# Two last stages of an attention-and-MLP kernel: the order of seven products per unit, the accumulators of the next unit, and the tile of one sum

## The chip, the cores and the metric

The kernel runs on one core of one Trainium2 chip. The metric is the device time of one launch in microseconds (us). A core has five engines that run side by side and meet only through semaphores: TensorE (PE) for matrix products, VectorE (DVE), ScalarE (ACT), GpSimd (POOL), and SyncE (SP), which here only issues transfers. [...]

## The reference, cut to what matters

Eight batches of eight heads (576 positions, head dimension 64) go through an attention with a forgetting gate; the 4608 rows of 512 values that come out go through an MLP of 2048 hidden features with a tanh GELU.

```python
attn = softmax(scale * q @ k.T + decay, causal)     # per batch and head
x    = (attn @ v)  as [4608, 512]
h    = x @ w_in                                     # [4608, 2048]
g    = 0.5 * h * (1 + tanh(c * (h + 0.044715 * h**3)))
out  = g @ w_out                                    # [4608, 512]
```

## The kernel before

The rows are worked in nine chunks of 512, numbered 0 to 8. For each chunk there are an input half (`x @ w_in` and GELU, into the tile `gT`) and an output half (`g @ w_out`, `seven_products`, lines from 554). Attention for later rows is interleaved with the MLP of earlier ones. The order of all work is written out by hand: `TABLES[c]` holds one string for chunk c, whose words are played from left to right, and each engine runs its instructions in the order in which they are issued. From chunk 7 on no attention is left: the tables of chunks 7 and 8 hold only MLP work.

The words that matter here:

- `F.n`, `O.n`: the next n steps of the output half of this chunk, or of the chunk before (a step is one matmul; `f.n` plays each as four narrow ones).
- `P.pr` and `p.pr`: the input half of a pair of feature tiles by plain products (eight matmuls of 512 columns); `p` plays it in two halves of four matmuls, the second with its GELU (lines 384 to 392). It has a PSUM tile of its own.
- `R.k.act`: the next step of unit k (`seven_in`, a generator; each `yield` ends a step). In chunks 7 and 8 three units, 1, 0 and 3, run one after the other, all with act 1.
- `T`: `x_sums` for the next chunk, four DVE subtractions (line 406) that make the operands t1 to t4.
- `K.k.n` and `k.k.n`: one of the four sums of weights of unit k (`w_sums`, line 421), on DVE or on POOL. The fourth overwrites a block of `w_in_sb` and is the operand s3.
- `G`: sums of parts of `gT` on DVE for the output half. `D`: softmax denominators (a transpose, a reciprocal, a transpose, on DVE).

A unit makes four output blocks (two feature tiles by 256 columns each) with seven products of four matmuls instead of eight. I name the products by the accumulator: `pa` and `pb` come from the pool `psS` (two slots), `pc` and `pd` from `psM` (two slots).

| name | product | line that issues it | what follows, and on which engine |
|---|---|---|---|
| A1 | a11 b11 into `pa` | 444 | P: ACT copies `pa` to SBUF, 447 |
| B | s2 t2 into `pb` | 451 | U = pb + P on DVE, 452 |
| C1 | s1 t1 into `pc` | 453 | V = pc + U on DVE, 454 |
| D1 | s3 t3 into `pd` | 455 | W = pd + V on DVE, 456; GELU of W on ACT, 462 |
| A2 | a12 b21 added into `pa` | 459 | GELU straight from `pa` on ACT, 460 |
| C2 | s4 b22 added into `pc` | 463 | X = pc + U on DVE, 464; GELU of X, 477 |
| D2 | a22 t4 added into `pd` | 468 | Y = pd + U on DVE, 474; GELU of Y, 480 |

C2 and D2 accumulate onto what C1 and D1 left, so C2 may start only when V has read `pc`, D2 only when W has read `pd`, and A2 only when P has been copied. U, V and W are a chain on DVE. X is written into P's tile and Y into U's tile, so Y waits for X. The number on a name is its unit's (W0 is W of unit 0, P3 the copy of unit 3). In the profile the matmuls of all products have the line 433, all GELUs of a unit 442. H0 and H1 are the two halves of `p.2`, between products of the units; `p.6` gives two more around unit 3's last two products.

The order on PE in chunk 7 is: A1 B C1 D1 A2 (unit 1), H0, C2 D2 (unit 1), A1 B C1 D1 A2 (unit 0), H1, C2 D2 (unit 0), A1 B C1 D1 A2 (unit 3), a half of `p.6`, C2, D2, the other half, then the output half. ACT's order around unit 0 and 3 is: GELU of A2 of unit 0, GELU of the pair of `p.2`, GELU of W0, copy P3, GELU of X0 and Y0, and so on. In chunk 8 unit 1's A1 is issued ahead of the last ten matmuls of chunk 7's output half; all else is as in chunk 7.

The pool `psS` gives a new tile the slot that has been free longest. Built, unit 0's `pa` lies in the bank that unit 1's `pb` had, and its `pb` in that of unit 1's `pa`; unit 3's are turned once more.

Of the kernel before, what the change touches and what calls it, by code (L numbers as in the profile page):

```python
# [16 lines left out]
def kernel(  # L17
# [10 lines left out]
    nc = tc.nc  # L28

    B, H, S, D = q.shape  # L30
# [76 lines left out]
    """  # L107
    TABLES[6] = """
        Y O.512 P.0.1 R.1 P.4.1 R.1 R.1 LK.q5 LQ.q5 M.q2.2 LV R.3.4 P.2.1 R.3 R.3 G.0.1.2 P.6 R.3 G.0.3.4 K.0.0 K.0.1 K.0.2 G.1.1.2 X F.10 S.q3.0 D.q2
        M.q3.0 f.22 S.q3.1 V.q2.0 M.q3.1 VW.q3 f.18 S.q3.2 V.q2.1 M.q3.2 cl.q3 k.0.3 f.20 D.q3 f.18 V.q3.0 v.q3.1 T f.14  # L110
    """
    TABLES[7] = """
        Y O.512 R.1.1 R.1 p.2 R.1 R.1 R.0.1 R.1 R.0 p.2 R.0 R.0 R.3.1 R.0 R.3 p.6 R.3 R.3 p.6 R.3 G.0.1.2 G.1.1.2 G.0.3.4 F.40 T
    """
    TABLES[8] = """
        O.62 R.1.1 O.512 R.1 p.2 R.1 R.1 R.0.1 R.1 R.0 p.2 R.0 R.0 R.3.1 R.0 R.3 p.6 R.3 R.3 p.6 R.3 G.0.1.2 G.1.1.2 G.0.3.4
    """

    singles = ctx.enter_context(tc.tile_pool(name="singles", bufs=1))
# [8 lines left out]
    def many(n, shape, dtype, name):  # L128
        return [singles.tile(shape, dtype, name=f"{name}{i}") for i in range(n)]
# [16 lines left out]
    u1, u2, u4 = many(3, [128, HF, HD], BF16, "usum")  # L146
# [249 lines left out]
    def x_blocks(c):  # L396

        new, old = xT[:, :, CH * c:CH * (c + 1)], xT[:, :, CH * (c - 1):CH * c]
        return [z[:, 2 * a:2 * a + 2, HC * b:HC * (b + 1)] for z in (new, old) for a in range(2) for b in range(2)]

    def x_sums(c, which, eng):

        b11, b12, b21, b22, t1, t2, t3, t4 = x_blocks(c)
        todo = ((t1, b12, b11), (t2, b22, t1), (t4, b21, t2), (t3, b22, b12))
        for k in which:
            eng.tensor_sub(*todo[k])

    def w_blocks(k):

        n = 256  # L410
        a11, a12, a21, a22 = (w_in_sb[:, 2 * b:2 * b + 2, HU * a + n * k:HU * a + n * (k + 1)]
                              for a in range(2) for b in range(2))
        old = xT[:, :, CH * HOMES[k]:CH * (HOMES[k] + 1)]
        return a11, a12, a21, a22, old[:, 0:2, 0:n], old[:, 0:2, n:], old[:, 2:4, 0:n]
# [5 lines left out]
        for n in which or range(4):  # L420
            (eng.tensor_sub if n else eng.tensor_add)(*todo[n])

    def seven_in(c, k, act=0):

        a11, a12, s3, a22, s1, s2, s4 = w_blocks(k)
        b11, b12, b21, b22, t1, t2, t3, t4 = x_blocks(c)
        pa, pb = (psS.tile([128, 2, 512], FP32, name="ps_ab", tag="s")[:, 0].rearrange("p (j n) -> p j n", j=2) for _ in range(2))
        pc, pd = (psM.tile([128, 2, HC], FP32, name="ps_cd", tag="m") for _ in range(2))

        def multiply(ps, w, x, first):  # L430
            for j in range(2):
                for dt in range(2):
                    nc.tensor.matmul(ps[:, j], w[:, dt, 128 * j:128 * j + 128], x[:, dt],  # L433
                                     start=(first and j == 0 and dt == 0), stop=(dt == 1),
                                     skip_group_check=True)

        def part():
            return snap_pool.tile([128, 2, HC], FP32, name="snap", tag="snap")

        def gelu(i, j, x):  # L440
            ft = N_FT // 2 * i + 2 * k
            nc.scalar.activation(gT[:, ft:ft + 2, HC * j:HC * (j + 1)], x, AF.Gelu_apprx_tanh)  # L442

        multiply(pa, a11, b11, True)
        p1, u2, v4 = part(), part(), part()
        if act in (1, 2, 3):
            nc.scalar.copy(p1, pa)
            yield
        else:
            nc.vector.tensor_copy(p1, pa)  # L450
        multiply(pb, s2, t2, True)
        nc.vector.tensor_add(u2, pb, p1)
        multiply(pc, s1, t1, True)
        nc.vector.tensor_add(v4, pc, u2)
        multiply(pd, s3, t3, True)
        nc.vector.tensor_add(v4, pd, v4)  # L456
        if act == 4:
            yield
        multiply(pa, a12, b21, False)
        gelu(0, 0, pa)  # L460
        yield
        gelu(1, 1, v4)
        multiply(pc, s4, b22, False)
        nc.vector.tensor_add(p1, pc, u2)
        if act in (0, 3, 4):
            gelu(0, 1, p1)
        yield
        multiply(pd, a22, t4, False)
        if act == 2:
            z = part()  # L470
            nc.scalar.copy(z, pd)
            nc.gpsimd.tensor_add(u2, z, u2)
        else:
            nc.vector.tensor_add(u2, pd, u2)
        if act in (1, 2):
            yield
            gelu(0, 1, p1)
        if act == 2:
            yield
        gelu(1, 0, u2)  # L480
        yield

    def mlp_in_half(half, g, spare=0):
# [252 lines left out]
    def load_values(b, half):  # L736
# [41 lines left out]
        "f": lambda c, n: out_part(c, n, 1),  # L778
        "K": lambda k, *which: w_sums(k, nc.vector, which),
        "T": lambda c, *which: x_sums(c, which or range(4), nc.vector),  # L780
        "B": keep_busy,
        "X": load_exp,
# [16 lines left out]
    def quads(call):  # L799
# [7 lines left out]
        "f": lambda c, n: out_part(c, n, 1),  # L807
        "P": lambda c, pr, spare=0: mlp_in(c, (pr,), spare),
        "R": lambda c, k, *how: next(units.setdefault((c, k), seven_in(c, k, *how))),
        "p": lambda c, pr: next(halves.setdefault((c, pr), mlp_in_halves(c, pr))),  # L810
        "TT": lambda c, *which: x_sums(c, which or range(4), nc.vector),
        "T": lambda c, *which: x_sums(c + 1, which or range(4), nc.vector),
        "t": lambda c, *which: x_sums(c + 1, which or range(4), nc.gpsimd),
        "G": lambda c, half, *which: gelu_sums(half, which or (1, 3, 2, 4)),
# [48 lines left out]
```

## Time and profile before

| what | value |
|---|---|
| median of 3 runs | 320.69 us (320.36 to 320.79) |
| the profiled execution | 320.23 us, span 318.5 us, mean granted TensorE clock 0.999 |
| PE, DVE, ACT, POOL busy, share of the span | 98%, 79%, 65%, 36% |
| chunk 7, from unit 1's A1 to the output half | 263.88 to 277.27 us |
| chunk 8, from unit 1's B to the output half | 289.94 to 302.53 us |

Times within the span count from its start. A row of the timeline gives the start, the duration, the engine, the line and the tiles of an instruction or of several equal ones in a row (x4). A matmul of 256 columns is shown with 0.27 us, though the next one starts 0.109 us later, because matmuls are pipelined: whether PE stood still is read from the distance of starts and not from its busy share. Four such matmuls, one product, take 0.4365 us from start to start (264.31, 264.75, 265.19 for three products in a row), four of 512 columns 0.865 us.

### The profile page before, as it was taken

What the parts mean: (1) busy time and instruction counts of PE and PEld (TensorE: products, weight loads), DVE (VectorE), ACT (ScalarE), POOL (GpSimd) and SP (SyncE); (2) the same over time, 40 slices, a digit from 0 to 9 for tenths busy, and PEclk for the clock granted to TensorE, in tenths of its full rate; (3) what the DMA queues carried; (4) which work ended last, traced back from release to release, by engine and by line L of the source; (5) the groups of instructions that cost most, each with busy time, mean ns of one, the idle gap of its engine ahead of it and who ended that gap; (6) DMA issues with size and microseconds to landing.
All of it is one profiled execution on the core that took longest, in us unless ns stands there. A gap on an engine that the chain in (4) does not pass through costs nothing.

```text
span 318.5 us, 12369 instructions
## 1 busy us (share of the span) xinstructions
PE 310.9 (98%) x5533; PEld 218.8 (69%) x5553; DVE 251.5 (79%) x402; ACT 206.1 (65%) x260; POOL 115.2 (36%) x163
## 2 busy tenths in 40 slices
PE   7999999999999999999999999999999999999995
PEld 3468744445876577767867777768776798788784
DVE  6877059877788999779977999689868978886882
ACT  4894767677756786659665965778477834722730
POOL 8996476910500229501870078105710350000000
PEclk9999999999999999999999999999999999999999
DMA  7999999898114820791159413961120111003013
GB/s 128 226 209 192 206 217 234 160 204 177 37 37 121 142 65 7 155 227 19 37 104 212 87 37 81 182 140 37 37 68 0 37 39 66 3 33 102 0 35 99
DMA packets 47574, 33.45 MB, mean 105 GB/s; under 512 B 29857, under 2 KB 42273, under 8 KB 47521
## 3 DMA queue, kind: packets, MB, share of 16 engines
q0 software_dynamic: 9712, 15.99, 29.2%
q1 hardware_dynamic: 37664, 16.60, 19.7%
q8 instruction: 43, 0.70, 1.0%
q14 instruction: 11, 0.08, 0.1%
q10 hardware_dynamic: 144, 0.07, 0.1%
HBM read 36.85 MB, written 9.44 MB: 145 GB/s over the span
## 4 chain that ended last, share of the span: by engine, by line
PE 94%; DMA 2%; DVE 1%; issue 1%; ACT 1%; POOL 0%; DVEq 0%; ACTq 0%; POOLq 0%
PE ps_w L567 30%; PE ps_h L374 16%; PE po L329 9%; PE ps_s L262 9%; PE ps_cd L433 8%; PE ps_ab L433 6%; PE pso L639 4%; PE ps_h L493 4%; PE ps_h L388 2%; DMA q_c<-in_q_dram 2%; PE po_m L315 1%; PE ps_q L516 1%; ACT pt L270 1%; PE idle_ps L240 1%; PE ps_o L329 0%
## 5 line engine op out<-in xcount | busy, mean ns | idle before, releaser
L270 ACT ACTIVATE pt<-ps_s 128x1024 bf16<-128x1024 f32 (+2 forms) x98 | 92.3, 992 | 36.2 <-PE ps_s L262 32.7
L276 POOL TENSOR_SCALAR_AFFINE_SELECT pt<-pt 128x512 bf16<-128x512 bf16 (+2 forms) x69 | 41.0, 603 | 102.9 <-ACT pt L270 101.8
L374 PE MATMUL ps_h<-xT,w_in_sb 128*128 128x512 bf16 x228 | 54.5, 379 | 0.6
L567 PEld LDWEIGHTS <-gT 128*32 128x32 bf16 (+1 forms) x1247 | 50.5, 97 | 6.1 <-issue 1.7
L567 PE MATMUL ps_w<-w_out_sb,gT 128*32 128x256 bf16 (+1 forms) x1050 | 46.9, 273 | 0.0
L381 ACT ACTIVATE gT<-ps_h 128x1024 bf16<-128x1024 f32 x30 | 30.6, 1021 | 19.5 <-PE ps_h L374 19.2
L567 PEld LDWEIGHTS <-gsum 128*32 128x32 bf16 (+1 forms) x1256 | 39.2, 97 | 1.4
L374 PEld LDWEIGHTS <-w_in_sb 128*128 128x128 bf16 x240 | 23.4, 98 | 24.3 <-issue 0.4
L262 PE MATMUL ps_s<-qT,kT 32*128 32x448 bf16 (+5 forms) x880 | 35.3, 261 | 0.3 <-DVE qT L198 0.2
L215 POOL TENSOR_TENSOR vw<-v_nat,wT 128x1280 bf16<-128x1280 f32 (+1 forms) x13 | 29.8, 2292 | 3.2 <-DVE xT L360 2.8
L567 PE MATMUL ps_w<-usum,gsum 128*32 128x256 bf16 (+1 forms) x832 | 30.6, 273 | 0.0
L198 DVE STREAM_TRANSPOSE kT<-k_c 128x576 f32<-128x576 f32 x16 | 19.9, 1243 | 11.6 <-DMA k_c<-in_k_dram 11.6
L592 DVE TENSOR_TENSOR o_st<-ps_w,snap 128x512 f32<-128x512 f32 x31 | 21.2, 686 | 8.8 <-PE ps_w L567 7.7
L433 PEld LDWEIGHTS <-w_in_sb 128*128 128x128 bf16 x240 | 23.4, 98 | 6.7 <-issue 1.0
L442 ACT ACTIVATE gT<-snap 128x512 bf16<-128x512 f32 x45 | 26.1, 626 | 2.9 <-DVE snap L456 2.4
L262 PEld LDWEIGHTS <-kT 32*128 32x128 bf16 x896 | 16.0, 92 | 17.1 <-issue 12.2
L329 PE MATMUL po<-pt,vw 128*32 128x64 bf16 (+4 forms) x624 | 22.6, 278 | 0.0
L360 DVE TENSOR_TENSOR xT<-po,rb 128x576 bf16<-128x576 f32 x26 | 19.5, 751 | 3.1 <-PE po L329 2.7
L329 PEld LDWEIGHTS <-vw 128*32 128x32 bf16 x672 | 14.2, 97 | 10.4 <-issue 4.1
L433 PEld LDWEIGHTS <-xT 128*128 128x128 bf16 x180 | 17.6, 98 | 4.4
L198 DVE STREAM_TRANSPOSE qT<-q_c 128x576 f32<-128x576 f32 x16 | 19.9, 1245 | 0.7 <-DMA q_c<-in_q_dram 0.6
L433 PE MATMUL ps_cd<-xT,w_in_sb 128*128 128x256 bf16 x120 | 18.0, 272 | 0.3 <-DVE snap L456 0.3
(112 smaller groups left out, 475.3 us busy)
## 6 DMA issues: line engine op xcount, KB each, us to landing
out_dram<-o_st SPq DMA_DIRECT2D x35, 256.0 KB, 2.6
k_c<-in_k_dram POOLq DMA_DIRECT2D x16, 288.0 KB, 5.9
q_c<-in_q_dram POOLq DMA_DIRECT2D x16, 288.0 KB, 7.1
v_nat<-in_v_dram SPq DMA_DIRECT2D x16, 256.0 KB, 6.5
v_nat<-in_v_dram SPq DMA_DIRECT2D x20, 128.0 KB, 5.6
w_in_sb<-in_moe_w_in_dram POOLq DMA_DIRECT2D x8, 256.0 KB, 6.7
w_out_sb<-in_moe_w_out_dram POOLq DMA_DIRECT2D x4, 512.0 KB, 10.2
v_nat<-in_v_dram POOLq DMA_DIRECT2D x9, 128.0 KB, 7.9
```

The source lines that it names most:

```text
L198: nc.vector.transpose(out=dst.rearrange("p s c -> p (s c)").bitcast(FP32) .rearrange("p (t a) -> p a t", a=S // 32), in_=src.rearrange("p ...
L215: return eng.tensor_mul(vw[i % 2][:, t0:t1], vb[:, t0:t1, h0:h0 + 4, :], wT[:, i, t0:t1, :].unsqueeze(3).to_broadcast([128, t1 - t0, 4, D]))
L262: nc.tensor.matmul(tiles[h // 2][:, h % 2, c0:c0 + nq], key_columns(i, key, h, c), qq[32 * h:32 * h + 32, q0:q0 + nq, c], start=(c == 0 an ...
L270: nc.scalar.activation(p[:, 2 * g:2 * g + 2, off:off + n], t[:, :, 0:n], AF.Exp, scale=scale)
L276: nc.gpsimd.affine_select(out=x, in_=x, compare_op=ALU.is_ge, fill=0.0, base=0, pattern=pattern, channel_multiplier=-1)
L329: nc.tensor.matmul(po[r0:r0 + w.shape[-1], 448 + q0:448 + q0 + nq], w, p[:, h, col:col + nq], start=(key in (0, "low")), stop=(key in ("lo ...
L374: nc.tensor.matmul(ph[:, j, :], w_in_sb[:, dt, 128 * ft:128 * ft + 128], xT[:, dt, CH * c:CH * (c + 1)], start=(dt == 0), stop=(dt == N_DT ...
L381: nc.scalar.activation(gT[:, 2 * pr:2 * pr + 2, :], ph, AF.Gelu_apprx_tanh)
L433: nc.tensor.matmul(ps[:, j], w[:, dt, 128 * j:128 * j + 128], x[:, dt], start=(first and j == 0 and dt == 0), stop=(dt == 1), skip_group_c ...
L442: nc.scalar.activation(gT[:, ft:ft + 2, HC * j:HC * (j + 1)], x, AF.Gelu_apprx_tanh)
L567: nc.tensor.matmul(ps[c0:c0 + width, n, cols[0]:cols[1]], x[:, j, 128 * n + c0:128 * n + c0 + width], w[:, j, cols[0]:cols[1]], start=(fir ...
L592: nc.vector.tensor_add(st, ps, kept[name])
```

## The change

Six edits, of which the first four concern chunks 7 and 8 (act 1) alone:

1. In a unit, A2 and its GELU are issued ahead of D1 and W.
2. P and U share a tile (U is written over P); X and Y each have a tile of their own, so Y no longer waits for X.
3. Unit 0's A1, with its copy, is issued between unit 1's C2 and D2, and unit 3's between unit 0's C2 and D2.
4. Unit 0 swaps the names of its two `psS` tiles. Built, every accumulator lies in the same bank as before.
5. In all chunks, `x_sums` makes t3 third and t4 fourth (before: t4 third, t3 fourth).
6. In chunk 6, the fourth weight sum of unit 0 moves from POOL to DVE and behind 20 steps of the output half; on DVE it stands between an addition of the output half (line 592) and the transpose of a denominator (line 348).

```diff
@@ TABLES[6], the second line
-        ... M.q3.2 cl.q3 k.0.3 f.20 D.q3 f.18 V.q3.0 v.q3.1 T f.14
+        ... M.q3.2 cl.q3 f.20 K.0.3 D.q3 f.18 V.q3.0 v.q3.1 T f.14
@@ TABLES[7]
-        Y O.512 R.1.1 R.1 p.2 R.1 R.1 R.0.1 R.1 R.0 p.2 R.0 R.0 R.3.1 R.0 R.3 p.6 R.3 R.3 p.6 R.3 G.0.1.2 G.1.1.2 G.0.3.4 F.40 T
+        Y O.512 R.1.1 R.1 p.2 R.1 R.0.1.1 R.1 R.1 R.0 p.2 R.0 R.3.1 R.0 R.0 R.3 p.6 R.3 R.3 p.6 R.3 G.0.1.2 G.1.1.2 G.0.3.4 F.40 T
@@ TABLES[8]
-        O.62 R.1.1 O.512 R.1 p.2 R.1 R.1 R.0.1 R.1 R.0 p.2 R.0 R.0 R.3.1 R.0 R.3 p.6 ...
+        O.62 R.1.1 O.512 R.1 p.2 R.1 R.0.1.1 R.1 R.1 R.0 p.2 R.0 R.3.1 R.0 R.0 R.3 p.6 ...
@@ x_sums
-        todo = ((t1, b12, b11), (t2, b22, t1), (t4, b21, t2), (t3, b22, b12))
+        todo = ((t1, b12, b11), (t2, b22, t1), (t3, b22, b12), (t4, b21, t2))
@@ seven_in
-    def seven_in(c, k, act=0):
+    def seven_in(c, k, act=0, swapped=0):
...
+        if swapped:
+            pa, pb = pb, pa
...
         multiply(pa, a11, b11, True)
-        p1, u2, v4 = part(), part(), part()
+        p1 = part()
+        u2, v4 = (p1, None) if act == 1 else (part(), part())
...
         multiply(pc, s1, t1, True)
+        v4 = v4 or part()
         nc.vector.tensor_add(v4, pc, u2)
+        if act == 1:
+            multiply(pa, a12, b21, False)
+            gelu(0, 0, pa)
         multiply(pd, s3, t3, True)
         nc.vector.tensor_add(v4, pd, v4)
         if act == 4:
             yield
-        multiply(pa, a12, b21, False)
-        gelu(0, 0, pa)
+        if act != 1:
+            multiply(pa, a12, b21, False)
+            gelu(0, 0, pa)
         yield
         gelu(1, 1, v4)
         multiply(pc, s4, b22, False)
-        nc.vector.tensor_add(p1, pc, u2)
+        c12 = part() if act == 1 else p1
+        nc.vector.tensor_add(c12, pc, u2)
...
         multiply(pd, a22, t4, False)
...
-            nc.vector.tensor_add(u2, pd, u2)
+            c21 = part() if act == 1 else u2
+            nc.vector.tensor_add(c21, pd, u2)
```

The number of matmuls, of weight loads and of transfers is the same, and so is ACT's order. DVE has one instruction more and POOL one less.

More of the change, by code (lines that the diff above doesn't have):

```diff
@@ L109 @@
         Y O.512 P.0.1 R.1 P.4.1 R.1 R.1 LK.q5 LQ.q5 M.q2.2 LV R.3.4 P.2.1 R.3 R.3 G.0.1.2 P.6 R.3 G.0.3.4 K.0.0 K.0.1 K.0.2 G.1.1.2 X F.10 S.q3.0 D.q2
-        M.q3.0 f.22 S.q3.1 V.q2.0 M.q3.1 VW.q3 f.18 S.q3.2 V.q2.1 M.q3.2 cl.q3 k.0.3 f.20 D.q3 f.18 V.q3.0 v.q3.1 T f.14
+        M.q3.0 f.22 S.q3.1 V.q2.0 M.q3.1 VW.q3 f.18 S.q3.2 V.q2.1 M.q3.2 cl.q3 f.20 K.0.3 D.q3 f.18 V.q3.0 v.q3.1 T f.14
     """
     TABLES[7] = """
-        Y O.512 R.1.1 R.1 p.2 R.1 R.1 R.0.1 R.1 R.0 p.2 R.0 R.0 R.3.1 R.0 R.3 p.6 R.3 R.3 p.6 R.3 G.0.1.2 G.1.1.2 G.0.3.4 F.40 T
+        Y O.512 R.1.1 R.1 p.2 R.1 R.0.1.1 R.1 R.1 R.0 p.2 R.0 R.3.1 R.0 R.0 R.3 p.6 R.3 R.3 p.6 R.3 G.0.1.2 G.1.1.2 G.0.3.4 F.40 T
     """
     TABLES[8] = """
-        O.62 R.1.1 O.512 R.1 p.2 R.1 R.1 R.0.1 R.1 R.0 p.2 R.0 R.0 R.3.1 R.0 R.3 p.6 R.3 R.3 p.6 R.3 G.0.1.2 G.1.1.2 G.0.3.4
+        O.62 R.1.1 O.512 R.1 p.2 R.1 R.0.1.1 R.1 R.1 R.0 p.2 R.0 R.3.1 R.0 R.0 R.3 p.6 R.3 R.3 p.6 R.3 G.0.1.2 G.1.1.2 G.0.3.4
     """
@@ L463, in seven_in @@
         multiply(pc, s4, b22, False)
-        nc.vector.tensor_add(p1, pc, u2)
+        c12 = part() if act == 1 else p1
+        nc.vector.tensor_add(c12, pc, u2)
         if act in (0, 3, 4):
-            gelu(0, 1, p1)
+            gelu(0, 1, c12)
         yield
@@ L471, in seven_in @@
             nc.scalar.copy(z, pd)
-            nc.gpsimd.tensor_add(u2, z, u2)
-        else:
-            nc.vector.tensor_add(u2, pd, u2)
+            c21 = u2
+            nc.gpsimd.tensor_add(c21, z, u2)
+        else:
+            c21 = part() if act == 1 else u2
+            nc.vector.tensor_add(c21, pd, u2)
         if act in (1, 2):
             yield
-            gelu(0, 1, p1)
+            gelu(0, 1, c12)
         if act == 2:
             yield
-        gelu(1, 0, u2)
+        gelu(1, 0, c21)
         yield
```

## The prediction

> **What bounds the kernel now.** I read the shares of the engines first, then the chain that ended last, then the timelines of PE, ACT and DVE in chunks 7 and 8, where the change lies.
>
> The page's busy times and, from the chain, the one stretch of chunks 7 and 8 that is not PE:
>
> ```profile
> PE 310.9 (98%) x5533; PEld 218.8 (69%) x5553; DVE 251.5 (79%) x402; ACT 206.1 (65%) x260; POOL 115.2 (36%) x163
> ...
> 270.25 0.88 PE ps_h L388 x4
> 271.15 0.70 DVE snap L456
> 272.50 0.87 PE ps_ab L433 x8
> ```
>
> PE carries the chain, so only time in which PE stands still can be won, and the reader should see that there is little. Work without a gap in chunk 7 would be 21 products of 0.4365 us and four halves of 0.865 us, 12.63 us; it took 277.27 - 263.88 = 13.39. Chunk 8 from unit 1's B: 20 products and four halves, 12.19 us, against 302.53 - 289.94 = 12.59. So 0.76 and 0.40 us, 1.16 in all, is the most that the order can give.
>
> Where it lies, in chunk 7, from the timelines of PE, ACT and DVE (H1, C2 and D2 of unit 0; GELU of the pair, GELU of W0, copy P3; then V0, W0, X0):
>
> ```profile
> 270.08 1.03 PE L388 MATMUL ps_h<-xT,w_in_sb 128*128 128x512 bf16 x4
> 270.95 0.60 PE L433 MATMUL ps_cd<-xT 128*128 128x256 bf16 x4
> 271.90 0.60 PE L433 MATMUL ps_cd<-xT,w_in_sb 128*128 128x256 bf16 x4 [0.35 <-DVE snap L456]
> ...
> 271.15 1.02 ACT L391 ACTIVATE gT<-ps_h 128x1024 bf16<-128x1024 f32 x1 [0.27 <-PE ps_h L388]
> 272.07 0.62 ACT L442 ACTIVATE gT<-snap 128x512 bf16<-128x512 f32 x1
> 273.02 0.59 ACT L447 COPY snap<-ps_ab 128x512 f32<-128x512 f32 x1 [0.33 <-PE ps_ab L433]
> ...
> 270.01 0.69 DVE L454 TENSOR_TENSOR snap<-ps_cd,snap 128x512 f32<-128x512 f32 x1
> 271.15 0.69 DVE L456 TENSOR_TENSOR snap<-ps_cd,snap 128x512 f32<-128x512 f32 x1 [0.46 <-PE ps_h L388]
> 271.76 0.68 DVE L464 TENSOR_TENSOR snap<-ps_cd,snap 128x512 f32<-128x512 f32 x1
> ```
>
> D2 of unit 0 starts 0.95 us after C2 instead of 0.44: it waits for W0. W0 starts 1.14 us after V0; everywhere else a sum that needs the one before starts 0.80 us after it. It should have started at 270.81, and D1, which it reads, ended at 269.81. The page blames H1, which W0 does not read. I take this as a late start of 0.34 us that I can't explain.
>
> The same stretch and the rest of chunk 8, where no sum starts late (C2 and D2 of unit 0; C2, D2 of unit 3; then ACT: pair, W0, P3; then U3, V3, W3):
>
> ```profile
> 296.55 0.60 PE L433 MATMUL ps_cd<-xT 128*128 128x256 bf16 x4
> 297.15 0.60 PE L433 MATMUL ps_cd<-xT,w_in_sb 128*128 128x256 bf16 x4
> ...
> 300.63 0.60 PE L433 MATMUL ps_cd<-xT 128*128 128x256 bf16 x4
> 301.23 0.60 PE L433 MATMUL ps_cd<-xT,w_in_sb 128*128 128x256 bf16 x4
> ...
> 296.75 1.02 ACT L391 ACTIVATE gT<-ps_h 128x1024 bf16<-128x1024 f32 x1 [0.27 <-PE ps_h L388]
> 297.67 0.62 ACT L442 ACTIVATE gT<-snap 128x512 bf16<-128x512 f32 x1
> 298.28 0.59 ACT L447 COPY snap<-ps_ab 128x512 f32<-128x512 f32 x1
> ...
> 298.89 0.69 DVE L452 TENSOR_TENSOR snap<-ps_ab,snap 128x512 f32<-128x512 f32 x1 [0.22 <-ACT snap L447]
> 299.69 0.69 DVE L454 TENSOR_TENSOR snap<-ps_cd,snap 128x512 f32<-128x512 f32 x1
> 300.49 0.69 DVE L456 TENSOR_TENSOR snap<-ps_cd,snap 128x512 f32<-128x512 f32 x1
> ```
>
> This is what decides. Each D2 starts 0.60 after its C2, so PE stands 0.16 us before each; but unit 3's D2 hangs on a chain that begins at H1: H1 at 295.69, GELU of the pair 1.06 later, GELU of W0 0.92 later, P3 0.61, U3 0.61, V3 0.80, W3 0.80, D2 0.74. From H1 to the output half it is 302.53 - 295.69 = 6.84 us, and PE has slack in all of it. A hole that is closed between H1 and that D2 opens again in front of it.
>
> **The change part by part.**
>
> *Unit 1's part.* The products ahead of H1 are the same before and after: twelve and H0. Ahead of it before, chunk 7: D2 of unit 1 waits for W1 (starts at 266.92 and 267.47 for C2 and D2, 0.11 us of standing). Afterwards unit 0's A1 lies between them, D2 comes 0.44 us later, and W1, limited by the sums U, V, W and not by D1, is no later (D1 would end at 266.23, and W1 starts at 266.72 as before). The hole goes: H1 at 269.99 for 270.08, 0.09 us. In chunk 8 D1 waits 0.07 us for an addition of the output half (starts 290.37, 290.88) and D2 0.02; A2 ahead of D1 covers the one and A1 the other: 0.09 us.
>
> *A2 ahead of D1.* A2 adds onto `pa` and so waits for copy P. Unit 1 in chunk 7: P from 264.51 to 265.10, and A2 would now start at 265.19. The slack is 0.09 less the hand-over, for which the nearest row is DVE to PE, W1's end at 267.41 to D2 at 267.47: 0.06. Cost nothing, with 0.03 to spare; bounds 0 and 0.3 (the 0.35 us that D2 above stood). In unit 0 the margin is 0.4 us. In unit 3 it is negative: P3, behind two GELUs on ACT, ends about 272.5 + 0.6, and A2 would come at 273.05. About 0.1 us of standing, which costs nothing, as W3 follows the chain of sums and not D1 (D1 ends half a microsecond before it).
>
> *A1 between C2 and D2.* It closes the 0.51 and 0.16 us ahead of unit 0's D2, but what follows is bound by the chain from H1. P3 no longer needs to wait for A1's end: in chunk 7 it started at 273.02, because A1, behind the late D2, started at 272.33. Afterwards P3 follows the GELU of W0 by 0.61 us as in chunk 8, or by 0.53 as two GELUs in a row do (1.15 us for two of 0.62). Late next is unit 3's D2, as in chunk 8, 0.15 us.
>
> *Own tiles for X and Y.* Y follows X by 0.61 us and not 0.80. PE covers it on both sides: Y starts when D2 ends, and U of the next unit waits for P. Nothing; if PE were faster, 0.19 us per unit. The rows show no wait for a `snap` tile, and six buffers for four tiles a unit leave each free for a unit and a half.
>
> *t3 ahead of t4.* The four subtractions took 1.67 us with two that wait for the one before; now one does, some 0.1 us less of DVE. They end at 263.7, two sums of the output half follow, and U1 waits for P1 in any case. 0 to 0.1 us per chunk, taken as 0.
>
> *The weight sum on DVE.* DVE sums of this shape took 0.42 us (line 421 at 247.28), POOL 1.16. DVE has a hole there:
>
> ```profile
> 256.77 0.69 DVE L592 TENSOR_TENSOR o_st<-ps_w,snap 128x512 f32<-128x512 f32 x1 [0.84 <-PE ps_w L567]
> 258.04 0.78 DVE L348 STREAM_TRANSPOSE den<-po 128x576 f32<-128x576 f32 x1 [0.58 <-PE po L329]
> ...
> 257.64 0.39 POOL L220 COPY vw<-vw 64x256 bf16<-64x256 bf16 x1
> 258.11 1.16 POOL L421 TENSOR_TENSOR w_in_sb<-w_in_sb 128x512 bf16<-128x512 bf16 x1
> ```
>
> It would run from 257.38 to 257.80, before the transpose. Cost nothing. If POOL's work beside it held it up to 258.03, the transpose would be 0.4 late; 0.18 is taken up by the next wait for PE (260.68), the rest by the 0.36 us by which the addition at 263.63 is done before C1 at 264.75. Nothing still. POOL has no later work, and nobody then waits for POOL: unit 0's D1, which did, reads a sum seven microseconds old.
>
> The trace shows such a hold-up the other way round: a POOL mask at 253.08 took 0.95 us beside a DVE sum of two SBUF tiles, against 0.61 for its like. [...]
>
> *Sum.* After the change both chunks go by the chain: H1 plus 6.84, or 6.76 with the shorter P3. Chunk 7: 269.99 + 6.84 = 276.83, against 277.27: 0.44 (0.52). Chunk 8: H1 at 295.60 for 295.69: 0.09 (0.17). Together 0.53 to 0.69, and 0.34 of it is the late W0, which the new order would swallow (D2 comes 0.44 us later there). If it is a matter of that one execution, the change is worth 0.19 to 0.35.
>
> Against the profiled execution's own time, 320.23, that is 319.6. The median, 320.69, is 0.46 higher, and nothing says whether it has the late start in it: with it 320.1, without it 320.4. I take 320.3, 0.4 us below the median.
>
> **The rivals.** A measurement of this kernel tells about 0.2%, 0.64 us, from no change.
>
> *More is won.* For it: PE stands 1.16 us in these chunks, and a late W0 in each run leaves 0.53 to 0.69 already. Against it: the chain from H1 is untouched. With the upper sum and half of the two remaining holes of 0.15, about 0.85 us: 319.8; all holes gone, 319.5. Chance 0.21.
>
> *The holes only move.* The late W0 isn't there in other runs, A2 waits 0.1 us for P1, and what is won at H1 is lost: 320.6 to 320.7. For it: 0.03 us of margin. Chance 0.16.
>
> *Slower: A2 behind the copy.* A2 now follows P by one product less. If the hand-over from ACT to PE were not 0.06 but more, unit 1's A2 in chunk 7, and with it H1 and the whole chain, would be late by all above 0.09; from 0.3 on it eats what is won, and at 1.1 us the kernel is 0.8 us slower, 321.5. Against it: no row has so long a hand-over; ACT's result at the start of the kernel (5.08) was taken up by PE at 5.19. Chance, together with a shift elsewhere in the program, 0.08.
>
> **How the numbers follow.** My forecast, 0.2 to 0.6 us less, has 0.55, its own range 320.05 to 320.5. Faster by over 0.2% is the first rival, 0.21; slower the third, 0.08; within, the forecast and the second, 0.71. The range that leaves out 2 in 10 reaches from 319.7, into the first rival, to 320.9, above the second by the spread of the runs (0.2 either side of the median).
>
> **What would show it.** H1 6.1 us after unit 1's A1 in chunk 7; D2 of units 1 and 0 right behind A1 of the next, with no wait for W; P3 right behind the GELU of W0 on ACT; a hole of about 0.1 us before unit 3's A2 and one of 0.15 before its D2; chunk 7 at 12.95 us and chunk 8 at 12.5. I am wrong if unit 3's sums start before the GELU of W0 ends, if A2 of unit 1 stands, or if a late start of a sum as W0's turns up in U3, V3 or W3, where nothing swallows it.

## The result and the profile after

The changed kernel takes 319.83 us (median of 16 runs, 319.29 to 321.3), the kernel before 320.55 us in the same comparison (16 runs, 320.22 to 321.54). The ratio is 0.9977 with a 95% interval of 0.9967 to 0.9987: 0.23% faster, 0.72 us by the medians. The profiled execution took 320.07 us, with a span of 318.4 us; it was one of the slower ones, as its chunk 7 began at 264.49 us, 0.61 later than in the profile before. That start moves by itself: the interleaving alone, below, edits nothing ahead of chunk 7 and begins it at 264.37. What the change did is therefore read from the two stages and not from the span.

| stage | before | after | won |
|---|---|---|---|
| chunk 7, unit 1's A1 to the output half | 13.40 | 12.85 | 0.55 |
| chunk 7's output half, to chunk 8's B | 12.66 | 12.66 | 0 |
| chunk 8, unit 1's B to the output half | 12.59 | 12.41 | 0.18 |
| chunk 8's output half, to the last matmul's end | 12.48 | 12.48 | 0 |

The sum, 0.73 us, agrees with the 0.72 us between the medians. In the twelve profiles that follow, a stage repeats to 0.01 us where its order of work is the same and a sum starts late in the same place or in none, while chunk 7 begins anywhere from 263.85 to 266.93 us; a stage's length in one profile shows what ten runs of the whole barely show.

From PE's timeline in chunk 7, H1, then C2 of unit 0, A1 of unit 3, D2 of unit 0:

```profile
270.60 1.03 PE L388 MATMUL ps_h<-xT,w_in_sb 128*128 128x512 bf16 x4
271.46 0.60 PE L435 MATMUL ps_cd<-xT 128*128 128x256 bf16 x4
271.90 0.60 PE L435 MATMUL ps_ab<-xT,w_in_sb 128*128 128x256 bf16 x4
272.34 0.60 PE L435 MATMUL ps_cd<-xT,w_in_sb 128*128 128x256 bf16 x4
```

The starts are 0.86, 0.44 and 0.44 us apart: no hole is left here, where PE had stood 0.51 us. H1 starts 6.11 us after unit 1's A1, for 6.20 before. The same stretch on DVE (V0, W0) and on ACT (GELU of the pair, GELU of W0, copy P3):

```profile
270.45 0.69 DVE L458 TENSOR_TENSOR snap<-ps_cd,snap 128x512 f32<-128x512 f32 x1
271.59 0.69 DVE L463 TENSOR_TENSOR snap<-ps_cd,snap 128x512 f32<-128x512 f32 x1 [0.46 <-DVE snap L458]
...
271.66 1.02 ACT L391 ACTIVATE gT<-ps_h 128x1024 bf16<-128x1024 f32 x1 [0.70 <-PE ps_h L388]
272.58 0.62 ACT L444 ACTIVATE gT<-snap 128x512 bf16<-128x512 f32 x1
273.10 0.58 ACT L450 COPY snap<-ps_ab 128x512 f32<-128x512 f32 x1
```

W0 is late again, by the same 0.34 us (1.14 after V0), so it is no accident of one execution. But D2, which waits for it, now comes at 272.34 in any case, and the GELU of W0 stands behind that of the pair. P3 follows the GELU of W0 by 0.52 us.

What is left of standing is in unit 3: its C1 and A2, then its C2 and D2.

```profile
273.21 0.60 PE L435 MATMUL ps_cd<-xT 128*128 128x256 bf16 x4
273.73 0.60 PE L435 MATMUL ps_ab<-xT,w_in_sb 128*128 128x256 bf16 x4
...
275.46 0.60 PE L435 MATMUL ps_cd<-xT 128*128 128x256 bf16 x4
276.05 0.60 PE L435 MATMUL ps_cd<-xT,w_in_sb 128*128 128x256 bf16 x4
```

Each second product starts more than 0.4365 us after the first: 0.08 more before A2, which waits for P3, and 0.15 more before D2, which waits for W3. In chunk 8 the same two holes stand.

### The profile page after: what moved, and what is told of

Its sections match the earlier page's. It is cut to its first block, busy times and chain, and to the rows that moved or that the text cites. A ratio compares the mean times of both kernels' runs of the same rounds, so it can differ in the third digit from the quotient of the medians.

```text
span 318.4 us, 12381 instructions
## 1 busy us (share of the span) xinstructions
PE 312.1 (98%) x5553; PEld 218.9 (69%) x5553; DVE 250.8 (79%) x403; ACT 205.8 (65%) x260; POOL 114.3 (36%) x162
## 4 chain that ended last, share of the span: by engine, by line
PE 94%; DMA 2%; DVE 1%; issue 1%; ACT 1%; POOL 0%; DVEq 0%; ACTq 0%; POOLq 0%
PE ps_w L578 30%; PE ps_h L374 16%; PE ps_s L262 9%; PE po L329 9%; PE ps_cd L435 8%; PE ps_ab L435 6%; PE pso L650 5%; PE ps_h L504 4%; PE ps_h L388 2%; DMA q_c<-in_q_dram 2%; PE po_m L315 1%; PE ps_q L527 1%; ACT pt L270 1%; PE idle_ps L240 1%; PE ps_o L329 0%
## 5 line engine op out<-in xcount | busy, mean ns | idle before, releaser
L192 POOL DMA_DIRECT2D k_c<-in_k_dram x16 | 9.2, 578 | 25.0 <-DVE qT L198 20.8
```

## The experiments

They were to settle three questions: which edit wins the time; whether the chain from H1 is what now bounds the stage; and what the late start of W0 is. For each kernel the table gives the two stages from its profile and the times of whole runs; where a ratio is given, it is against the kernel before, which ran again beside each experiment. Its medians there were 320.60 us (for the interleaving, the unit's order and tiles, the sums' edits and the pair's GELU late), 320.70 (for the changed kernel with six fewer and the three kernels with 30 more) and 320.57 (for the rest), so medians of different groups are compared with care.

| kernel | chunk 7 | chunk 8 | median | ratio, 95% interval |
|---|---|---|---|---|
| before | 13.40 | 12.59 | 320.55 | |
| changed | 12.85 | 12.41 | 319.83 | 0.9977 (0.9967 to 0.9987) |
| interleaving alone | 12.92 | 12.55 | 320.11 | 0.9987 (0.9975 to 1.0) |
| unit's order and tiles alone | 13.36 | 12.59 | 320.66 | 1.0004 (0.9975 to 1.0034) |
| sums' edits alone | 13.05 | 12.59 | 320.17 | 0.9987 (0.9978 to 0.9995) |
| t3 first alone (one run) | 13.40 | 12.59 | 320.25 | |
| before, one DVE instruction more | 13.05 | 12.59 | 319.94 | 0.9985 (0.9974 to 0.9996) |
| before, two more (one run) | 13.39 | 12.59 | 320.53 | |
| before, 30 more | 13.05 | 12.59 | 320.39 | 0.9993 (0.997 to 1.0016) |
| changed, 30 more | 12.85 | 12.41 | 320.23 | 0.9975 (0.9961 to 0.9989) |
| changed, six fewer | 13.20 | 12.41 | 322.63 | 1.0059 (1.0037 to 1.008) |
| changed, pair's GELU late | 12.71 | 12.27 | 319.61 | 0.9968 (0.9956 to 0.998) |
| the same, 30 more | 12.71 | 12.27 | 319.65 | 0.9965 (0.9952 to 0.9978) |
| the same, both halves of `p.6` early | 13.13 | 12.69 | 320.38 | 0.999 (0.9982 to 0.9999) |

**The interleaving alone.**

```diff
-  TABLES[7]: R.1.1 R.1 p.2 R.1 R.1 R.0.1 R.1 R.0 p.2 R.0 R.0 R.3.1 R.0 R.3 ...
+  TABLES[7]: R.1.1 R.1 p.2 R.1 R.0.1.1 R.1 R.1 R.0 p.2 R.0 R.3.1 R.0 R.0 R.3 ...
   (TABLES[8] alike)
...
+        if swapped:
+            pa, pb = pb, pa
```

> The kernel before with edits 3 and 4 alone (the next unit's A1 between C2 and D2, names swapped). Theory 1 (chain from H1): A1 in between closes unit 1's hole before D2, takes the late W0 off PE's path, and lets P3 follow the GELU of W0; chunk 7 goes from 13.39 to about 12.86 us and chunk 8 from 12.59 to about 12.5 (D1's 0.07 us there stays): 0.55 to 0.7 us less in all. Rival (the products within a unit and the own tiles bring it): at most 0.2 us less.

Measured: chunk 7 12.92, chunk 8 12.55, 0.52 us won of the 0.73. Chunk 7 is 0.07 short of the changed kernel: with the order within a unit as before, D1 of unit 0 comes right behind C1 and waits for Y1, which reads the same bank and starts only when unit 1's D2, now one product later, is done (C1 and D1 from PE's timeline, Y1 from DVE's):

```profile
269.16 0.60 PE L435 MATMUL ps_cd<-xT 128*128 128x256 bf16 x4
269.67 0.60 PE L435 MATMUL ps_cd<-xT,w_in_sb 128*128 128x256 bf16 x4
...
268.93 0.69 DVE L476 TENSOR_TENSOR snap<-ps_cd,snap 128x512 f32<-128x512 f32 x1 [0.18 <-PE ps_cd L435]
```

C1 and D1 are 0.51 us apart for 0.44. X1 ended at 268.74, so Y1 waited for D2 and not for X1: it is A2 ahead of D1, and not the own tiles, that covers this hole. So the first theory holds for the larger part, if a little short of its 0.55 us, and edits 1 and 2 are worth 0.07 and 0.14 us beside the interleaving (in chunk 8 unit 1's D1 still stands 0.07 us as well).

**The order and the tiles of a unit alone.**

```diff
+        if act == 1:
+            multiply(pa, a12, b21, False)
+            gelu(0, 0, pa)
         multiply(pd, s3, t3, True)
   (and the tiles of the diff; the tables, x_sums and the weight sum as before)
+  FRONT: ... TK.2 N.1 X ...        # one DVE write of a number that nobody reads
```

> The kernel before with edits 1 and 2 alone (A2 ahead of D1, own tiles for X and Y), no interleaving; one tiny DVE instruction is added in the first stage, so that W0 stays the same instruction by number on DVE. Theory 1: only the 0.07 us before chunk 8's D1 goes; chunk 7 stays at 13.3 to 13.4 us: 0 to 0.15 us less. Rival (these edits bring it): 0.4 us less or more.

Measured: 13.36 and 12.59. The 0.07 us before chunk 8's D1 went, but did not shorten the stage: D2 of unit 1 now stands 0.09 us for W1 in place of 0.02 (C2 at 292.99, D2 at 293.52), so H1 comes no earlier, and the chain from H1 sets the end. Alone these edits are worth 0.04 us, beside the interleaving 0.21.

**The sums' edits alone, and then the order of the subtractions by itself.**

```diff
-        todo = ((t1, b12, b11), (t2, b22, t1), (t4, b21, t2), (t3, b22, b12))
+        todo = ((t1, b12, b11), (t2, b22, t1), (t3, b22, b12), (t4, b21, t2))
-  TABLES[6]: ... cl.q3 k.0.3 f.20 D.q3 ...       # this part not in the second kernel
+  TABLES[6]: ... cl.q3 f.20 K.0.3 D.q3 ...
```

> The kernel before with edits 5 and 6 alone (t3 ahead of t4, the fourth weight sum on DVE). Theory 1: DVE has room for both; 0 us within 0.1, chunks 7 and 8 as before. Rival (the DVE time that these edits move is worth something in the earlier chunks, or costs something): 0.2 us or more either way.

> The kernel before with edit 5 alone (t3 ahead of t4), which leaves the count of DVE instructions as it was. Theory 1: chunk 7 at 13.40 us, W0 late as before, so that the 0.35 us that edits 5 and 6 won came from the one instruction that edit 6 adds on DVE. Rival (the order of the subtractions wins it): 13.05 us.

The first one surprised me: chunk 7 took 13.05 us and not 13.40. The second gave 13.40. Neither the subtractions nor the weight sum lie in chunk 7's path, but the weight sum adds one instruction to DVE ahead of it. Here W0 first came without its late start.

**One, two and thirty DVE instructions more in the kernel before.**

```diff
+    filler = singles.tile([1, 64], FP32, name="filler")
-  FRONT: ... LQ.4 TK.2 X F.0.7 ...
+  FRONT: ... LQ.4 TK.2 N.n X F.0.7 ...           # n = 1, 2, 30
+        "N": lambda n: [nc.vector.memset(filler[:, j:j + 1], 0.0) for j in range(n)],
```

> The kernel before with 30 tiny DVE instructions (writes of one number each to a tile that nobody reads) added in the first stage, where DVE stands idle for 10 us. Theory 1 (the late start of W0 belongs to the place in DVE's instruction stream: the same record, the 448th of DVE, starts 0.34 us late in both profiles, and the one 256 records earlier has a like gap): it now falls on the transpose of a denominator in chunk 6, which waits for PE anyway; W0 follows V0 by 0.80 us, chunk 7 takes 13.05 us for 13.39, 0.3 us less in all. Rival (it belongs to W0, to H1 or to the place in the program): W0 is late as before, no change.

> The kernel before with one tiny DVE instruction added in the first stage. Theory 1 (the late start belongs to DVE's 448th record): that record is now the instruction that waits for V0, which stands for 0.73 us in any case; W0 follows V0 by 0.80 us and chunk 7 takes 13.05 us for 13.40. Rival (the late start belongs to W0 or its place, and the two sums edits won 0.35 us by themselves): chunk 7 at 13.40 us.

> The kernel before with two such instructions. Theory 1: the 448th record is now V0, which starts 1.14 us after U0 and not 0.80; W0 and unit 0's D2 come as late as in the kernel before: chunk 7 at 13.40 us again. Rival (any added instruction removes it): 13.05 us.

By the stages all three came out as the first theory has it. The whole runs show it for one instruction more (0.9985, 0.9974 to 0.9996), while with thirty more their spread covers it (0.997 to 1.0016); W0 follows V0 by 0.80 us there too. DVE's timelines, U0, V0 and W0, with one instruction more:

```profile
269.19 0.69 DVE L453 TENSOR_TENSOR snap<-ps_ab,snap 128x512 f32<-128x512 f32 x1 [0.16 <-ACT snap L448]
269.98 0.69 DVE L455 TENSOR_TENSOR snap<-ps_cd,snap 128x512 f32<-128x512 f32 x1
270.78 0.69 DVE L457 TENSOR_TENSOR snap<-ps_cd,snap 128x512 f32<-128x512 f32 x1
```

and with two:

```profile
269.53 0.69 DVE L453 TENSOR_TENSOR snap<-ps_ab,snap 128x512 f32<-128x512 f32 x1 [0.16 <-ACT snap L448]
270.68 0.69 DVE L455 TENSOR_TENSOR snap<-ps_cd,snap 128x512 f32<-128x512 f32 x1 [0.46 <-PE ps_ab L434]
271.47 0.69 DVE L457 TENSOR_TENSOR snap<-ps_cd,snap 128x512 f32<-128x512 f32 x1
```

The steps are 0.80 and 0.80 with one, 1.15 and 0.80 with two: the late start has gone back to V0. Counted with the instructions that only wait for a semaphore, it is the 448th record of DVE in the trace that is late by 0.35 us, in the kernel before, in the changed one, and here. With one instruction more the 448th is itself only the wait for V0's end, and a late start of 0.35 us would be hidden in the 0.73 us for which that stands. A release by H1, as the timeline of before named it, is ruled out: with one instruction more W0 starts at 270.78, while H1, from 270.06 and 1.03 us long, is still running.

**The same thirty in the changed kernel, and six fewer.**

```diff
-            nc.vector.memset(t_[:, 0:64], 0.0)
-            nc.vector.memset(t_[:, 64 + S:], 0.0)
+            nc.gpsimd.memset(t_[:, 0:64], 0.0)
+            nc.gpsimd.memset(t_[:, 64 + S:], 0.0)
...
-            nc.vector.memset(t_[0:64, LOW, :, :], 0.0)
+            nc.gpsimd.memset(t_[0:64, LOW, :, :], 0.0)
-            nc.vector.memset(t_[64:128, HIGH, :, :], 0.0)
+            nc.gpsimd.memset(t_[64:128, HIGH, :, :], 0.0)
```

> The changed kernel with the same 30 tiny DVE instructions. Theory 1: the late start leaves W0 for the weight sum of chunk 6, but the new order had swallowed it on W0: chunk 7 at 12.85 us as in the changed kernel, no change within 0.1 us; against the kernel before with the same 30 instructions only 0.3 to 0.4 us less. Rival (the late W0 still costs something in the changed kernel): chunk 7 0.1 to 0.3 us shorter than in the changed kernel.

> The changed kernel with some zero fills of the first microseconds on POOL instead of DVE, so that DVE's stream is six instructions shorter up to chunk 7. Theory 1: the late start falls on V3, in the chain of sums that unit 3's D2 waits for, where nothing swallows it: V3 follows U3 by 1.14 us and not 0.80, chunk 7 takes 13.2 us for 12.86, 0.3 us more than the changed kernel (apart from what the zero fills do at the start). Rival (bound to W0 or the place): W0 late as before, chunk 7 unchanged.

With thirty more, chunk 7 is 12.85 us as without: the late W0 costs the changed kernel nothing. The two kernels with thirty more give what the change is worth where no sum starts late: 13.05 to 12.85 us and 12.59 to 12.41, 0.38 us in the stages, as expected; the medians differ by 0.16. The 448th record is here the weight sum, and it is not late. It starts 0.61 us behind the addition before it, which started at 259.05, as it does in the changed kernel (257.39, 258.00), and takes the same 0.47 us:

```profile
259.65 0.47 DVE L422 TENSOR_TENSOR w_in_sb<-w_in_sb 128x512 bf16<-128x512 bf16 x1
```

With six fewer the 448th record is V3, in the one chain that has no slack (U3, V3, W3; here U3 and V3):

```profile
275.92 0.69 DVE L455 TENSOR_TENSOR snap<-ps_ab,snap 128x512 f32<-128x512 f32 x1
277.07 0.69 DVE L458 TENSOR_TENSOR snap<-ps_cd,snap 128x512 f32<-128x512 f32 x1 [0.46 <-PE ps_cd L435]
```

1.15 us from U3 to V3, and chunk 7 takes 13.20 us, all of the 0.35 more. The time of the whole is no measure here: chunk 7 starts 2.2 us later in this profile than in the changed kernel's, at 266.71, and the fills on POOL in the first microseconds are the only edit before it. How much of the longer run is theirs, no run separates: two profiles without these fills begin chunk 7 as late, at 266.15 and 266.93.

**The GELU of the pair behind P3, also with thirty more.**

```diff
     def mlp_in_halves(c, pr, late=0):
+            if j and late:
+                yield
             if j:
                 nc.scalar.activation(gT[:, 2 * pr:2 * pr + 2, :], ph, AF.Gelu_apprx_tanh)
-  TABLES[7]: ... p.2 R.1 R.0.1.1 R.1 R.1 R.0 p.2 R.0 R.3.1 R.0 R.0 ...
+  TABLES[7]: ... p.2.1 R.1 R.0.1.1 R.1 R.1 R.0 p.2 R.0 R.3.1 p.2 R.0 R.0 ...
   (TABLES[8] alike)
```

> The changed kernel, with the GELU of the pair (second half of p.2) issued on ACT behind the copy P3 and no longer ahead of the GELU of W0. Theory 1 (unit 3's D2 hangs on the chain pair GELU, W0 GELU, P3, U3, V3, W3 from H1): P3 starts 0.25 us sooner in chunk 7 and 0.5 us in chunk 8, U3 waits for B instead, and the holes of 0.08 before unit 3's A2 and 0.15 before its D2 close: 0.4 to 0.5 us less than the changed kernel, 319.4. Rival (the holes before A2 and D2 have another cause, or the half pair of p.6 waits for the late GELU to free its PSUM tile): no less than the changed kernel.

> The changed kernel with the GELU of the pair behind P3, and with the 30 tiny DVE instructions. Theory 1: with the pair's GELU late, P3 stands behind the GELU of W0 alone, so the late W0 delays P3; without it P3 starts when A1 is done; but U3 then waits for B in both: within 0.1 us of the kernel with the GELU late and no added instructions. Rival (the late W0 matters there): 0.15 to 0.3 us less than that.

The chain from H1 was the bound: 0.14 us goes from each chunk, 12.71 and 12.27, with or without the added instructions. From ACT's timeline (GELU of W0, P3; the pair's GELU follows from 275.75), PE's (C2 and D2 of unit 3) and DVE's (Y0, U3):

```profile
274.75 0.63 ACT L446 ACTIVATE gT<-snap 128x512 bf16<-128x512 f32 x1 [1.36 <-DVE snap L465]
275.29 0.57 ACT L452 COPY snap<-ps_ab 128x512 f32<-128x512 f32 x1
...
277.81 0.60 PE L437 MATMUL ps_cd<-xT 128*128 128x256 bf16 x4
278.34 0.60 PE L437 MATMUL ps_cd<-xT,w_in_sb 128*128 128x256 bf16 x4
...
275.40 0.69 DVE L487 TENSOR_TENSOR snap<-ps_cd,snap 128x512 f32<-128x512 f32 x1
276.01 0.68 DVE L457 TENSOR_TENSOR snap<-ps_ab,snap 128x512 f32<-128x512 f32 x1
```

The size was off: I had expected 0.4 to 0.5 us and 0.28 came. Of the 0.22 us of standing in each chunk (12.85 less the 12.63 of work without a gap) 0.14 went, and 0.09 stays before D2. I had expected U3 to wait for B, but B, from 275.20 and 0.60 us long, is done before: U3 stands behind Y0, which starts as unit 0's D2 ends, and follows it by 0.61 us, here and in chunk 8. From unit 0's D2 on, Y0, U3, V3, W3 and the hand-over take longer than the products in between. Both kernels have lower medians than the changed one, 319.61 and 319.65 for 319.83, but they ran in other groups and the intervals of their ratios overlap its own, so it is the stages that show it.

**Both halves of `p.6` ahead of unit 3's C2 and D2.**

```diff
-  TABLES[7]: ... R.3 p.6 R.3 R.3 p.6 R.3 ...
+  TABLES[7]: ... R.3 p.6 p.6 R.3 R.3 R.3 ...
   (TABLES[8] alike; on top of the pair's GELU late)
```

> The kernel with the GELU of the pair behind P3, and both halves of p.6 ahead of unit 3's C2 and D2. Theory 1 (what is left there is the 0.09 us by which W3 is late for unit 3's D2): the second half covers it, chunk 7 at 12.63 us and chunk 8 at 12.19, no standing left, 0.15 to 0.2 us less than with the GELU late alone. Rival (the last GELUs and the sums behind them come too late for the output half, which then stands): the same or more, with a hole within the output half.

The rival's outcome came: 13.13 and 12.69, 0.42 us more in each chunk than before this edit. The hole before D2 closes, and a larger one opens at the output half (PE's C2, D2 and the first product of it):

```profile
275.93 0.60 PE L437 MATMUL ps_cd<-xT 128*128 128x256 bf16 x4
276.37 0.60 PE L437 MATMUL ps_cd<-xT,w_in_sb 128*128 128x256 bf16 x4
277.31 3.65 PE L580 MATMUL ps_w<-w_out_sb,gT 128*128 128x256 bf16 x32 [0.34 <-DVE snap L475]
```

The output half's first accumulator is the bank of `pc`, and X3 has to have read it. The second half of `p.6` between D2 and the output half had covered that wait; moved forward, it leaves 0.51 us of standing there.

## Why the prediction was right, point by point

- *Unit 1's part.* Right: H1 came 6.11 us after A1 in chunk 7, as forecast, and 5.67 after B in chunk 8 for 5.75; 0.09 and 0.08 us.
- *A2 ahead of D1.* Right: unit 1's A2 started at 265.80, right behind C1, no hole; in unit 3 it stood 0.08 us for P3, at no cost to the end, since W3 follows the chain. The hand-over from ACT to PE, for which I took 0.06 us from a DVE row, was 0.05 there (P3 ends at 273.68, A2 starts at 273.73). What I had not seen is that the interleaving by itself opens a hole of 0.07 us in each chunk, before unit 0's D1. Beside the interleaving this edit is therefore worth 0.21 us, and I had counted 0.07 of it, before unit 1's D1 in chunk 8.
- *Own tiles for X and Y.* I had put them at nothing, and no run shows otherwise: with the interleaving and without them, Y1 waits for D2 and not for X1. No run has them by themselves.
- *A1 between C2 and D2.* Right: D2 of units 1 and 0 follows with no wait, and the interleaving alone wins 0.52 us.
- *t3 ahead of t4.* Right: 13.40 and 12.59 with that edit alone.
- *The weight sum on DVE.* It ran from 258.00 to 258.47, ahead of the transpose at 258.66 that waits for PE, and cost nothing. By the rows it was not held up by POOL, whose two masks ran from 256.96 to 258.19: it started behind the DVE addition, 0.19 us before the second mask ended. The hold-up that the prediction weighs, to the end of POOL's copy (258.03 in the profile before), did not come for this pair. POOL's copy beside it took 0.47 us for 0.39, and the sum 0.47 for 0.42.
- *Sum.* The chain from H1 is what binds: 6.84 or 6.76 us forecast, 6.75 measured in both chunks. Chunk 7: 0.44 to 0.52 forecast, 0.55 measured; chunk 8: 0.09 to 0.17, and 0.18. The term that was mis-sized is the late W0: I put the forecast half-way between a late W0 in every run and in that one alone, at 0.4 us. It stands in every profile in which W0 is DVE's 448th record, so that the upper sum, 0.53 to 0.69, was the one to take, and 0.72 came. Without the late start the stages give 0.38 us, for 0.19 to 0.35 forecast.
- *The range.* My own interval, 320.05 to 320.5, missed the 319.83. The wide range, 319.7 to 320.9, holds it only because it reaches into the first rival, to which I gave 0.21; that it held is owed to that rival and to its width, and not to the forecast. Of the 0.47 us between 320.3 and 319.83, 0.14 is the kernel before, whose median is 320.55 in the comparison for 320.69 ahead of it, and the rest is the size of the change.
- *The rivals.* "More is won" is where the result fell, at its near edge: 0.72 us, with the lower of its two grounds (the late W0) and without the other (the holes before A2 and D2 stayed). A2 never waited for the hand-over in unit 1, so neither the second nor the third rival came.

## What to carry to other kernels

Where one engine carries the chain, follow the chain of the other engines from the last product that everybody waits for: a hole closed inside it opens again at its end (here the hole before unit 3's D2 closed, and PE stood 0.51 us at the output half), and it is the chain that has to be shortened (0.14 us a chunk with the pair's GELU behind P3). Here a stage that repeats to 0.01 us in the trace decides between orders that runs of the whole can't tell apart. An odd late start that stands in one profile is cheap to test: add an instruction or two on that engine well ahead, where it stands idle, and see whether it stays with the work or with the count.

## What the runs showed of the hardware that I had not expected

The 448th record of DVE's stream starts 0.35 us late where it is a sum right behind a wait that has just ended, whichever sum that is: W0 in both kernels (1.14 us after V0 for 0.80), V0 with two instructions more, V3 with six fewer. In the kernel before it costs the whole 0.35 us of the stage, half of what the change wins, and one idle instruction takes it away (0.9985, 0.9974 to 0.9996). Where the record is something else nothing of it is seen. With one more it is itself a wait that stands longer in any case (0.73 us), and with thirty more in the kernel before a transpose that waits for PE (0.58 us in the profile before). With thirty more in the changed kernel it is the weight sum, which starts while the addition before it still runs (at 259.65, with the addition from 259.05 0.69 us long), and no later than elsewhere. So not every instruction in that place is late; a delay that runs beside the instruction before it would look the same.

I had taken the record 256 earlier to have a like gap. The runs show none: the records around the 192nd start without a gap in the kernel before (the 192nd, a transpose, at 126.45, while the addition from 125.88, 0.65 us long, still runs), with thirty more and with six fewer. But in none of the kernels is the 192nd a sum right behind a wait that has just ended, so a late start like W0's could not have been seen there. What DVE waits for at the 448th record the runs don't show. It is a place in the stream that is late and not a piece of work, but no record of a transfer was tied to it: in the kernel before no DMA queue moves a packet from 269 to 272 us, around W0's start at 271.15. It stays open.
